# Softmaxed linear attention into an ELU feed-forward: the first two units' q in token halves, shares of their multiplies and casts on GpSimd, W1 loaded over 128 partitions, a new order table

## The chip, the cores and the metric

The kernel runs on one core of a Trainium2 chip. The core has a matrix engine (TensorE: PE, with its weight loads shown as PEld), three engines for elementwise work (VectorE: DVE; ScalarE: ACT; GpSimd: POOL), a sync engine (SP) that here only issues transfers, and 16 DMA engines that carry all transfers between the chip's memory (HBM) and the on-chip SBUF. PE writes its results to PSUM, eight banks of 512 float32 per partition; DVE and ACT read them there.

The metric is the device time in microseconds (us) of one execution: 300.37 us, the median of three runs (300.27 to 300.63).

## What is computed

The reference, cut to what matters. q, k and v have the shape (8 batches, 8 heads, 576 tokens, 64), w_in (512, 2048), w_out (2048, 512), all float32.

```
q_s = exp(q - max(q, over d));       q_s = q_s / sum(q_s, over d)
k_s = exp(k - max(k, over tokens));  k_s = k_s / sum(k_s, over tokens)
kv  = einsum('bhsd,bhse->bhde', k_s, v)
a   = einsum('bhsd,bhde->bhse', q_s, kv)
x   = a with its heads side by side: 4608 tokens x 512
h   = x @ w_in
g   = where(h > 0, h, exp(min(h, 0)) - 1)
out = g @ w_out
```

## The kernel before

**Units and blocks.** The attention is cut into 16 units, two for each batch: unit n holds four heads of batch n // 2. Its q, k and v are each one tile of 128 partitions by 2 x 9 x 64 float32 (1152 elements in a partition, 576 KB): two heads by nine chunks of tokens by 64 channels. The tokens, 4608 of them, are also cut into nine blocks of 512 for the feed-forward.

**A unit's steps.** ACT takes the exponential of q (L357). DVE sums it over the channels (L377), takes the reciprocal (L381) and multiplies (L385) into QS, in float16. PE transposes QS chunk by chunk (L408) into PSUM, from where ACT or DVE copies it to qsT (L415, L418). ACT takes the exponential of k (L361) and v is cast to bfloat16 into VB (L370 on ACT, L373 on DVE or GpSimd). PE multiplies the two into kv (L461, 36 small matmuls), DVE divides kv by the sums of k into MBLK (L470, L474), PE multiplies MBLK with qsT (L504 or L492, called "ao" below), and the result is copied into XT (L526 on ACT, L529 on DVE), the transposed x.

**The feed-forward.** W1 holds w_in as 128 partitions by four slices (kc) by 2048 columns, W2 holds w_out. For a block, eight groups g of 256 columns each take eight matmuls of 512 columns (L562: two halves by four slices kc), then exp on ACT (L578), and on ACT and DVE what makes the ELU of it (L589, L591, L595, L597), into GT. Four output tiles of a block each take sixteen matmuls against W2 (L607), a copy out of PSUM (L639) and two stores. The units of batch 0 come first, since all else needs them; the remaining units are worked off in between the matmuls of the blocks.

**The start.** `program` loads q, k, v of units 0 and 1 from SP in the order q0, k0, q1, v0, k1, v1. Ten loads of W1 go through GpSimd's queue, behind a gate: the first waits for the load of q1. Each fills 64 partitions, every second one, with rows of the upper or the lower half of w_in (`h`), for one, two or four slices kc: groups 0 to 2 for kc 0, kc 1 and kc 2 to 3, groups 3 to 4 and groups 5 to 7 for all kc. Behind them in the same queue come q2, W2 slices 0 and 1, q3, v2, k2, W2 slices 2 and 3, k3 and v3. While PE waits for the first units it runs spare matmuls on the identity (L687), from `SPIN_FROM` on.

**Order.** A planner records every operation with its reads and writes; the table ORDER, a list of operation numbers for each engine, says in which order each engine runs its operations, and the planner puts in the semaphore waits that the reads and writes ask for. An engine runs its list strictly in order: an operation that waits holds up all behind it. Durations in the code serve the planner's picture alone; on the chip the table and the waits decide.

Of the kernel before, what the change touches and what calls it, by code (L numbers as in the profile page):

```python
# [17 lines left out]
CH = 9  # L18
BYDMA = 4
CASTS = 6  # L20
CAST0, CAST1 = "act", "split"
# [3 lines left out]
        "30 32 34 47 45 49 50 53 71 73 74 58 57 72 75 77 80 78 81 76 79 82 92 96 103 125 113 100 139 "  # L25
        "138 146 147 140 148 117 141 149 119 160 159 136 161 144 166 142 168 162 167 150 169 163 156 "
        "183 185 182 184 243 249 248 247 254 253 202 255 261 259 260 266 211 267 213 273 272 265 222 "
        "271 278 277 279 323 319 230 331 343 335 327 348 360 344 290 339 292 401 409 356 301 352 422 "
        "309 405 427 361 448 418 410 489 414 372 423 431 435 374 440 436 444 383 510 449 391 493 515 "
        "497 498 506 502 460 536 462 519 523 511 528 574 471 532 524 479 595 582 578 537 587 600 591 "  # L30
        "583 548 621 608 613 550 604 596 646 559 617 609 654 650 566 622 667 672 659 655 680 663 632 "
        "693 668 634 676 698 681 689 685 719 642 706 644 702 694 711 724 715 732 707 737 728 720 745 "
        "741 750 733 771 758 754 746 763 776 759 767 784 772 789 780 785 797 793 798 802 803 807 815 "
        "811 819 "),
    "act": (
        "3 24 25 35 26 33 31 36 46 37 51 59 83 86 87 89 93 94 97 104 105 107 114 126 127 129 101 102 "
        "108 118 137 130 143 176 170 145 173 189 164 157 179 215 240 241 186 190 198 244 250 251 283 "
        "201 256 262 263 212 225 268 214 221 274 223 275 227 224 228 324 280 320 294 231 332 336 304 "
        "328 289 365 303 291 345 349 340 293 300 307 402 376 357 302 306 353 386 310 406 371 428 362 "
        "388 385 411 419 389 415 373 453 424 432 490 375 382 437 464 384 445 441 450 392 494 459 474 "  # L40
        "507 516 476 461 503 499 473 470 520 512 463 541 529 552 472 477 533 575 525 480 579 562 538 "
        "561 588 547 601 626 584 564 592 549 551 558 605 614 597 647 618 560 610 565 567 636 623 651 "
        "673 660 656 631 664 633 669 635 677 641 699 690 686 682 643 703 695 712 716 645 725 708 729 "
        "738 721 751 742 734 755 747 764 760 768 777 773 781 790 786 794 799 804 808 816 812 820 822 "),
    "dve": (
        "4 2 5 6 0 7 27 28 29 39 40 41 42 43 48 44 38 52 54 55 56 60 84 85 88 90 91 95 98 99 106 110 "
        "115 111 116 112 132 133 134 128 120 121 122 151 152 153 165 158 192 193 194 242 187 188 216 "
        "245 246 203 217 204 252 205 218 206 207 257 208 258 264 284 285 269 286 270 276 281 321 322 "
        "232 282 295 233 296 337 234 338 235 297 236 329 237 330 366 346 367 341 347 342 368 358 377 "
        "359 354 378 355 407 311 408 312 313 363 314 364 315 316 379 412 413 420 421 425 454 426 455 "  # L50
        "433 434 438 439 456 446 447 465 451 393 466 452 394 395 396 495 397 398 496 467 508 509 500 "
        "501 521 522 513 542 514 553 534 535 543 481 526 482 544 483 527 580 484 485 581 486 539 554 "
        "540 555 585 627 593 594 586 606 628 607 598 599 619 620 611 612 629 568 652 569 624 625 637 "
        "570 653 638 571 657 572 573 658 639 665 666 670 671 678 679 691 692 683 684 704 696 705 697 "
        "717 718 709 710 730 731 722 723 743 744 735 736 756 748 749 757 761 762 769 770 774 775 782 "
        "783 787 788 795 796 "),
    "gp": (
        "1 14 15 16 17 18 19 20 21 22 23 63 61 62 67 65 64 66 70 68 109 69 123 135 154 124 131 155 "
        "191 196 199 "),
    "sp": (  # L60
        "8 9 10 11 12 13 197 178 195 171 172 181 200 180 177 175 209 219 210 174 220 226 229 325 287 "
        "288 238 239 305 298 333 334 326 299 351 308 369 350 404 317 318 370 387 429 381 380 417 390 "
        "416 403 430 457 492 458 443 399 442 491 400 468 469 504 475 505 531 517 530 478 488 487 545 "
        "518 576 546 557 590 556 602 589 577 616 563 649 630 648 615 603 640 661 662 674 687 675 713 "
        "688 727 726 700 701 714 752 765 753 739 740 791 766 779 778 800 801 805 806 792 810 817 818 "
        "809 813 814 821 "),
# [17 lines left out]
class Sched:  # L84
# [5 lines left out]
    SPIN_FROM = 7900.0  # L90
# [154 lines left out]
class Gen:  # L245
# [67 lines left out]
    def load(self, n, t, key, eng="gp", follow=None):  # L313
        S = self.S
        b, u = n // 2, n % 2
        src = self.src[t][b].rearrange(
            "(h u f) (p c) d -> u (f p) h (c d)", h=2, u=2, c=CH)[u]
        tile, name = self.raw(t, n)
        dst = tile[:, :, :, :].rearrange("p h c d -> p h (c d)")
        S.add(eng, ISSUE[eng], lambda e: e.dma_start(dst, src), key, W=[name],  # L320
              dma=f"{name}{eng}", nbytes=128 * 4608,
              follow=self.gpq if eng == "gp" and n < 4 else follow)
        S.ops[-1].margin = 300 if n < 4 else 800
# [7 lines left out]
    def load_w1(self, g0, g1, kcs, key, after=()):  # L331
        w = self.w_in.rearrange("(h kc d) f -> h d kc f", h=2, d=D)
        sl = slice(g0 * 256, g1 * 256)
        ks = slice(kcs[0], kcs[-1] + 1)
        for h in range(2):
            self.S.add("gp", ISSUE["gp"], lambda e, h=h: e.dma_start(  # L336
                self.W1[h:128:2, ks, sl], w[h, :, ks, sl]), key,
                W=[f"W1_{g}{x}{h}" for x in kcs for g in range(g0, g1)],
                dma=f"w1{g0}{kcs[0]}{h}", nbytes=(len(kcs) * (g1 - g0) << 16) * (1.25 if g0 == 3 else 1), after=after,
                follow=self.gpq)  # L340
            self.gpq = self.S.ops[-1]
            self.gpq.margin = 600

    def load_w2(self, s, key, after=()):
        w = self.w_out.rearrange("(jj p) c -> p jj c", p=128)
        sl = slice(s * 4, (s + 1) * 4)
        self.S.add("gp", ISSUE["gp"], lambda e: e.dma_start(self.W2[:, sl, :], w[:, sl, :]), key,
                   W=[f"W2_{s}"], dma=f"w2{s}", nbytes=1 << 20, after=after, follow=self.gpq)

    def stage1(self, n, key, vconv="gp", what="qk"):  # L350
# [5 lines left out]
        if "q" in what:  # L356
            S.add("act", t_act(1152, False), lambda e: e.activation(flat(q), flat(q), AF.Exp),  # L357
                  key - 3, X=[f"qR{i}"], follow=self.table)
        if "k" in what:
# [4 lines left out]
            for eng, h0, h1, x in {"gp": [("gp", 0, 2, "")], "act": [("act", 0, 2, "")],  # L364
                                   "dve": [("dve", 0, 2, "")],
                                   "split": [("act", 0, 1, ""), ("dve", 1, 2, "x")]}[vconv]:
                dst, src = VB[:, h0:h1, :, 0:D], v[:, h0:h1, :, :]
                if eng == "act":
                    S.add("act", t_act(576 * (h1 - h0), False), lambda e, dst=dst, src=src:
                          e.activation(dst, src, AF.Copy), key - 50, R=[vname], W=[f"VB{i}{x}"])  # L370
                else:
                    S.add(eng, 1053 if eng == "gp" else t_dve(576 * (h1 - h0)),
                          lambda e, dst=dst, src=src: e.tensor_copy(dst, src), key - 50,  # L373
                          R=[vname], W=[f"VB{i}{x}"])
        if "q" not in what:
            return
        S.add("dve", t_dve(1152), lambda e: e.tensor_reduce(  # L377
            self.ZQ[i][:, :, :].rearrange("p h c -> p (h c)"),
            q[:, :, :, :].rearrange("p h c d -> p (h c) d"), AX.X, ALU.add),
            key - 3, R=[f"qR{i}"], W=[f"ZQ{i}"], follow=self.cleared)  # L380
        S.add("dve", 184, lambda e: e.reciprocal(self.RZQ[i][:, :, :], self.ZQ[i][:, :, :]),  # L381
              key - 3, R=[f"ZQ{i}"], W=[f"RZQ{i}"])
        rz = self.RZQ[i][:, :, :].unsqueeze(3).broadcast_to([128, 2, CH, D])
        qso = self.QS[self.alt(n)][:, :, :].rearrange("p c (h d) -> p h c d", h=2)
        S.add("dve", t_dve(1152), lambda e: e.tensor_tensor(  # L385
            qso, q[:, :, :, :], rz, ALU.mult),
            key - 3, R=[f"qR{i}", f"RZQ{i}"], W=[f"QS{self.alt(n)}"])
# [6 lines left out]
    def tp(self, n, ps, key, engs=("act", "act"), after=()):  # L394
# [7 lines left out]
        for (c0, c1, at, X, W), eng in zip(cuts, engs):  # L402
# [7 lines left out]
            S.add("pe", (c1 - c0) * 54 + 10, mm, key, R=[f"QS{self.alt(n)}", "ID"], X=X, side=1)  # L410
# [10 lines left out]
    def turn(self, n, key):  # L421
# [4 lines left out]
            key - 60, R=[f"QS{self.alt(n)}"], W=["QT"], dma="tq", nbytes=128 * 4608)  # L426
# [22 lines left out]
    KV = 382  # L449

    def kv_mm(self, n, ps, at=KV):
# [12 lines left out]
        return 615 if at == self.KV else 350, [f"kR{i}", f"VB{i}", f"VB{i}x", f"VBone{i}"], mm  # L464
# [73 lines left out]
    def early(self, g):  # L538

        names = [("QS1", 0, 2304), ("qsT10", 4096, 8704), ("qsT11", 4096, 8704),  # L540
# [6 lines left out]
    def hg_mm(self, j, g, ps, key, half=None, kc=None):  # L547
# [8 lines left out]
        ws = [f"W1_{g}{x}{h}" for x in kcs for h in range(2)]  # L556
# [97 lines left out]
    def program(self):  # L654
# [3 lines left out]
        self.gpq = None  # L658
        for n, t in ((0, "q"), (0, "k"), (1, "q"), (0, "v"), (1, "k"), (1, "v")):
            self.load(n, t, -40, "sp", follow=self.gpq)  # L660
            self.gpq = S.ops[-1]
            if (n, t) == (1, "q"):
                gate = S.ops[-1]
# [218 lines left out]
```

## Time and profile before

| what | value |
|---|---|
| median of three runs | 300.37 us |
| profiled execution, first to last instruction (its span) | 299.3 us |
| PE busy | 287.9 us (96%) |
| ACT, DVE, POOL busy | 181.3, 187.5, 22.8 us |
| first matmul against W1 (L562) | starts at 15.39 us |
| W1 loads issued on POOL | 8.65 to 14.7 us |
| moved by DMA in all | 49.96 MB |
| mean granted TensorE clock | 0.999 of full |

The page gives the profiled execution by its span; what of a run's time lies outside first to last instruction is the difference to the median, 1.07 us. Times in a timeline are us from the start of the span. A line of a group names line, engine, operation, the tiles written and read, the shape and the count, then busy time and the mean of one, then the engine's idle time just before and what ended it. The chain of waits is followed back from the last instruction: at each step to what released it. Line numbers are those of the kernel before; in the changed kernel the same code stands some lines lower (L562 becomes L576, L607 becomes L621, L336 becomes L339).

### The profile page before, as it was taken

To read this page: it belongs to the slowest core of one execution; us is meant where nothing else is said; L and a number is where in the kernel's file an instruction comes from. 1 tells how busy PE (TensorE), PEld (TensorE's weight loads), DVE (VectorE), ACT (ScalarE), POOL (GpSimd) and SP (SyncE) were. 2 spreads that over 40 slices of the span, in tenths; PEclk is the share of its full clock that TensorE was granted. 3 is DMA by queue.
4 is the path that set the end of the run, shared out by engine and by line. 5 is a ranking of instruction groups with operands and counts; after the bars stand their busy time and mean duration, and the time that the engine had idled before them with its cause. 6 is when DMAs were issued, how large, how long until landed. Compare 5 with 4: busy or idle time off the path is not lost.

```text
span 299.3 us, 4430 instructions
## 1 busy us (share of the span) xinstructions
PE 287.9 (96%) x1856; PEld 234.4 (78%) x1856; DVE 187.5 (63%) x244; ACT 181.3 (61%) x212; POOL 22.8 (8%) x35
## 2 busy tenths in 40 slices
PE   0999999999999999999999999999999999999995
PEld 0487877778888888888888888888888888888885
DVE  3858944997588767678468656749743654465500
ACT  5758749989788776674776576644553343334221
POOL 0880235100000000000000000000000000000000
PEclk9999999999999999999999999999999999999999
DMA  7999998997796795519626852450401130030433
GB/s 263 383 360 391 387 392 299 251 243 273 126 346 169 160 321 128 149 40 305 144 92 174 274 132 58 114 94 1 94 0 35 37 88 18 0 70 2 99 76 88
DMA packets 35475, 49.96 MB, mean 167 GB/s; under 512 B 16384, under 2 KB 16640, under 8 KB 35456
## 3 DMA queue, kind: packets, MB, share of 16 engines
q1 hardware_dynamic: 29840, 34.15, 41.8%
q0 software_dynamic: 5536, 15.47, 15.9%
q8 instruction: 14, 0.23, 0.3%
q10 hardware_dynamic: 80, 0.07, 0.1%
q14 instruction: 5, 0.04, 0.0%
HBM read 36.70 MB, written 9.44 MB: 154 GB/s over the span
## 4 chain that ended last, share of the span: by engine, by line
PE 84%; DMA 6%; DVE 4%; ACT 3%; POOL 2%; SPq 0%; issue 0%
PE PS L607 42%; PE PS L562 38%; DMA W<-in_moe_w_in_dram 4%; PE PS L492 2%; DMA QR<-in_q_dram 2%; POOL W L336 2%; PE PS L461 1%; DVE GT L597 1%; DVE GT L591 1%; ACT QR L357 1%; ACT OSBX L639 1%; DVE ESB L595 1%; DVE QS L385 0%; DVE ZQ L377 0%; ACT ESB L589 0%; DVE MBLK L474 0%
## 5 line engine op out<-in xcount | busy, mean ns | idle before, releaser
L562 PE MATMUL PS<-XT,W 128*128 128x512 f32 x576 | 139.8, 392 | 0.7 <-DVE GT L597 0.6
L607 PE MATMUL PS<-W,GT 128*128 128x512 f32 (+1 forms) x592 | 140.1, 386 | 0.0
L562 PEld LDWEIGHTS PS<-XT,W 128*128 128x128 f32 x576 | 106.8, 188 | 23.7 <-DVE GT L597 1.0
L607 PEld LDWEIGHTS PS<-W,GT 128*128 128x128 f32 x592 | 108.0, 188 | 21.6 <-DVE GT L591 0.3
L578 ACT ACTIVATE ESB<-PS 128x1024 f32<-128x1024 f32 x72 | 73.3, 1027 | 68.1 <-PE PS L562 67.6
L595 DVE TENSOR_SCALAR ESB<-ESB 128x1024 f32<-128x1024 f32 x64 | 44.2, 690 | 72.6 <-ACT ESB L578 72.4
L597 DVE TENSOR_TENSOR GT<-ESB,PS 128x1024 fp32r<-128x1024 f32 x64 | 77.5, 1215 | 1.6
L639 ACT ACTIVATE OSB<-PS 128x512 f32<-128x512 f32 x31 | 18.6, 599 | 23.3 <-PE PS L607 18.2
L526 ACT ACTIVATE XT<-PS 128x512 fp32r<-128x512 f32 (+6 forms) x32 | 19.4, 608 | 12.7 <-PE PS L492 7.7
L377 DVE TENSOR_REDUCE ZQ<-QR 128x18 f32<-128x1152 f32 x16 | 21.6, 1347 | 5.7 <-ACT QR L357 5.7
L385 DVE TENSOR_TENSOR QS<-QR,RZQ 128x1152 f16<-128x1152 f32 x16 | 21.6, 1352 | 0.8 <-PE PS L408 0.6
L357 ACT ACTIVATE QR<-QR 128x1152 f32<-128x1152 f32 x16 | 18.7, 1170 | 3.5 <-DMA QR<-in_q_dram 3.5
L361 ACT ACTIVATE KR<-KR 128x1152 bf16<-128x1152 f32 x16 | 18.3, 1161 | 2.5 <-DMA KR<-in_k_dram 2.5
L370 ACT ACTIVATE VB<-VR 128x1152 bf16<-128x1152 f32 (+1 forms) x12 | 13.5, 1124 | 1.7 <-PE PS L461 1.3
L436 ACT ACTIVATE qsT<-QT 128x1152 fp32r<-128x1152 f16 x12 | 14.0, 1170 | 0.0
L492 PEld LDWEIGHTS PS<-qsT,MBLK 128*128 128x128 f32 x60 | 11.0, 190 | 2.5 <-DVE MBLK L474 0.2
L492 PE MATMUL PS<-qsT,MBLK 128*128 128x320 f32 (+4 forms) x60 | 12.5, 296 | 0.0
L687 PE MATMUL PS<-ID 128*128 128x512 f16 x12 | 4.6, 508 | 7.3 <-ACT KR L361 7.3
L591 DVE SCALAR_TENSOR_TENSOR GT<-PS,ESB 128x1024 fp32r<-128x1024 f32 x8 | 9.8, 1222 | 2.8 <-ACT ESB L589 2.7
L474 DVE TENSOR_TENSOR MBLK<-PS,RZK 64x128 fp32r<-64x128 f32 x32 | 9.2, 286 | 0.7
L589 ACT ACTIVATE ESB<-ESB 128x1024 f32<-128x1024 f32 x8 | 8.5, 1059 | 0.2
L461 PEld LDWEIGHTS PS<-VB,KR 64*64 64x64 bf16 x576 | 5.7, 109 | 3.0 <-ACT VB L370 0.8
(31 smaller groups left out, 59.3 us busy)
## 6 DMA issues: line engine op xcount, KB each, us to landing
out_dram<-OSB SPq DMA_DIRECT2D x62, 128.0 KB, 2.4
QR<-in_q_dram SPq DMA_DIRECT2D x12, 576.0 KB, 4.5
KR<-in_k_dram SPq DMA_DIRECT2D x12, 576.0 KB, 5.7
VR<-in_v_dram SPq DMA_DIRECT2D x12, 576.0 KB, 4.6
W<-in_moe_w_out_dram POOLq DMA_DIRECT2D x4, 1024.0 KB, 18.4
QR<-in_q_dram POOLq DMA_DIRECT2D x4, 576.0 KB, 11.3
VR<-in_v_dram POOLq DMA_DIRECT2D x4, 576.0 KB, 9.6
KR<-in_k_dram POOLq DMA_DIRECT2D x4, 576.0 KB, 14.7
```

Source lines behind the costliest of these rows:

```text
L357: S.add("act", t_act(1152, False), lambda e: e.activation(flat(q), flat(q), AF.Exp), key - 3, X=[f"qR{i}"], follow=self.table)
L361: S.add("act", t_act(1152, False), lambda e: e.activation(ek[:, :, :, :].rearrange("p h c d -> p (h c d)"), flat(k), AF.Exp), key - 2, X=[ ...
L377: S.add("dve", t_dve(1152), lambda e: e.tensor_reduce(self.ZQ[i][:, :, :].rearrange("p h c -> p (h c)"), q[:, :, :, :].rearrange("p h c d ...
L385: S.add("dve", t_dve(1152), lambda e: e.tensor_tensor(qso, q[:, :, :, :], rz, ALU.mult), key - 3, R=[f"qR{i}", f"RZQ{i}"], W=[f"QS{self.al ...
L492: last = e.matmul(P[:, y:y + n_], M[:, f, :], T[:, c0:c1, f * 64:f * 64 + 64], start=True, stop=True)
L526: S.add("act", t_act((h1 - h0) * n_, True), lambda e, dst=dst, src=src: e.activation(dst, src, AF.Copy), key, W=W, X=X)
L562: last = e.matmul(P[:, t * 512:(t + 1) * 512], self.W1[:, kc, tt * 128:(tt + 1) * 128], self.XT[:, kc, rc:rc + BLK], start=(kc == 0), stop ...
L578: S.add("act", t_act(1024, True), lambda e: e.activation(esb[:, :], P[:, :], AF.Exp), key, W=[f"E{i}"], X=banks)
L595: S.add("dve", t_dve(1024, 2), lambda e: e.tensor_scalar(esb[:, :], esb[:, :], 1.0, -1.0, ALU.min, ALU.add), key, X=[f"E{i}"])
L597: S.add("dve", t_dve(1024), lambda e: e.tensor_tensor(gt, esb[:, :], P[:, :], ALU.max), key, R=[f"E{i}"], W=gw, X=banks)
L607: last = e.matmul(dst, GT[:, jj, ts * 128:(ts + 1) * 128], self.W2[:, jj, c0:c1], start=(jj == 0), stop=(jj == 15))
L639: S.add("act", t_act(512, True), lambda e: e.activation(osb[:, :], src, AF.Copy), key, W=[f"O{i}0", f"O{i}1"], X=[f"b{bk}"])
```

## The change

- The q of units 0 and 1 is worked in two parts: chunks 0 to 4 (640 elements in a partition) and 5 to 8 (512): exponential, sum, reciprocal and multiply each once for each part. The multiply of the second part runs on GpSimd. All later units keep one operation each.
- The v casts of units 0 and 1 are split by chunks: 0 to 4 on ACT, 5 to 8 on GpSimd. Before, ACT cast all of unit 0; ACT cast one head and DVE the other of unit 1.
- The first loads are issued in the order q0, q1, k0, v0, k1, v1, and the gate of the W1 loads is k0's load.
- W1 is loaded by twelve DMAs of 128 partitions, one slice kc each (384 KB for groups 0 to 2 and 5 to 7, 256 KB for 3 to 4). In each, neighbouring partitions hold rows of the upper and the lower half of w_in.
- In GpSimd's queue the two multiplies stand ahead of all W1 loads, the two casts between them; then W2 slice 0, q2, W2 slice 1, q3, k2, v2, W2 slices 2 and 3, the cast of v2, k3 and v3.
- The spare matmuls may begin at 5.5 us of the planner's time instead of 7.9, and the order table is a new one on every engine.

```diff
-CAST0, CAST1 = "act", "split"
+CAST0, CAST1 = "pair", "pair"
+XT0, XT1, TP0, TP1 = "both", "both", ("act", "act"), ("act", "dve")
...
-    SPIN_FROM = 7900.0
+    SPIN_FROM = 5500.0
...
+    HALF = ((0, 5), (5, CH))
...
     def load_w1(self, g0, g1, kcs, key, after=()):
-        w = self.w_in.rearrange("(h kc d) f -> h d kc f", h=2, d=D)
+        w = self.w_in.rearrange("(h kc d) f -> d h kc f", h=2, d=D)
         sl = slice(g0 * 256, g1 * 256)
-        ks = slice(kcs[0], kcs[-1] + 1)
-        for h in range(2):
-            self.S.add("gp", ISSUE["gp"], lambda e, h=h: e.dma_start(
-                self.W1[h:128:2, ks, sl], w[h, :, ks, sl]), key,
-                W=[f"W1_{g}{x}{h}" for x in kcs for g in range(g0, g1)],
...
+        for kc in kcs:
+            self.S.add("gp", ISSUE["gp"], lambda e, kc=kc: e.dma_start(
+                self.W1[:, kc, sl], w[:, :, kc, sl]), key,
+                W=[f"W1_{g}{kc}" for g in range(g0, g1)],
...
-                                   "split": [("act", 0, 1, ""), ("dve", 1, 2, "x")]}[vconv]:
-                dst, src = VB[:, h0:h1, :, 0:D], v[:, h0:h1, :, :]
+                                   "pair": [("act", 0, 5, ""), ("gp", 5, 9, "y")]}[vconv]:
+                if vconv == "pair":
+                    dst, src = VB[:, :, h0:h1, 0:D], v[:, :, h0:h1, :]
...
+        for c0, c1, xs in ([(c0, c1, [x]) for x, (c0, c1) in enumerate(self.HALF)]
+                           if n in self.HALVED else [(0, CH, [0, 1])]):
+            part, m = slice(c0, c1), (c1 - c0) * 128
+            qp, zp, rp = q[:, :, part, :], self.ZQ[i][:, :, part], self.RZQ[i][:, :, part]
+            if n in self.HALVED:
+                S.add("act", t_act(m, False), lambda e, qp=qp: e.activation(qp, qp, AF.Exp),
...
+            S.add("dve", t_dve(m), lambda e, qp=qp, zp=zp: e.tensor_reduce(zp, qp, AX.X, ALU.add),
...
+            S.add("dve", 184, lambda e, zp=zp, rp=rp: e.reciprocal(rp, zp),
...
+            eng = "gp" if n in self.HALVED and c0 else "dve"
+            S.add(eng, m * 2.2 + 80 if eng == "gp" else t_dve(m), lambda e, qp=qp, rz=rz, dst=qs[:, :, part, :]: e.tensor_tensor(
+                dst, qp, rz, ALU.mult),
...
+    HALVED = (0, 1)
...
-        for n, t in ((0, "q"), (0, "k"), (1, "q"), (0, "v"), (1, "k"), (1, "v")):
-            self.load(n, t, -40, "sp", follow=self.gpq)
-            self.gpq = S.ops[-1]
-            if (n, t) == (1, "q"):
+        for n, t in ((0, "q"), (1, "q"), (0, "k"), (0, "v"), (1, "k"), (1, "v")):
+            self.load(n, t, -40, "sp")
+            if (n, t) == (0, "k"):
                 gate = S.ops[-1]
-        loaded = S.ops[-1]
-        for g0, g1, kcs in ((0, 3, (0,)), (0, 3, (1,)), (0, 3, (2, 3)), (3, 5, range(4)), (5, 8, range(4))):
-            self.load_w1(g0, g1, kcs, -30, [gate, self.ident] if kcs == (0,) else ())
-            S.ops[-2].behind = loaded
+        self.load_w1(0, 3, (0,), -30, [gate])
+        self.load_w1(0, 3, (1, 2, 3), -30)
+        self.load_w1(3, 5, range(4), -30)
+        self.load_w1(5, 8, range(4), -30)
...
+        self.load(2, "q", -28)
         self.load_w2(0, -29)
         self.load_w2(1, -29)
-        for t in "qkv":
-            self.load(2, t, -28)
+        for n, t in ((2, "k"), (2, "v"), (3, "q")):
+            self.load(n, t, -28)
         self.load_w2(2, -27)
-        for t in "qkv":
+        self.load_w2(3, -25)
+        for t in "kv":
             self.load(3, t, -26)
-        self.load_w2(3, -25)
```

On the engines the new table gives this for the start. DVE sums q0's second part, q1's second part, q0's first, q1's first, then multiplies the two first parts. ACT takes the four exponentials, copies q0's second part out of PSUM, then k0, v0, k1, q0's first part, v1, the first XT copy, q1's first part, the next XT copy. PE transposes the second parts of units 0 and 1, the first part of unit 0, does unit 0's kv, transposes the first part of unit 1, ao of unit 0, kv of unit 1, four matmuls of W1's slice 0 (groups 0 and 1), ao of unit 1, and then slice by slice. Before, six matmuls of W1 (slices 0 and 1) stood ahead of ao of unit 1.

## The prediction

> **What bounds the kernel now.** I read the page's busy shares first, then the chain of waits in order of time up to 60 us, then the timeline of the first 22 us, then one-microsecond windows of the DMA rate, then the DMA issues.
>
> ```profile
> PE 287.9 (96%) x1856; PEld 234.4 (78%) x1856; DVE 187.5 (63%) x244; ACT 181.3 (61%) x212; POOL 22.8 (8%) x35
> ```
>
> PE is busy 96% of the span, and in the long middle (100 to 250 us) 100% at full clock. A gain can only come from where PE isn't yet on real work, or waits.
>
> ```profile
> 1.75 6.62 DMA QR<-in_q_dram
> 8.65 5.38 POOL W L336 x9
> 14.03 11.32 DMA W<-in_moe_w_in_dram
> 25.35 0.04 issue
> 25.39 5.74 PE PS L562 x24
> ...
> 53.85 1.22 DVE GT L591
> ...
> 56.93 1.26 DVE ZQ L377
> ...
> 58.83 1.22 DVE GT L597
> ```
>
> Start and length in us. The chain of the first 25 us isn't arithmetic: it is q of unit 1 landing (the gate of the W1 loads), nine W1 issues on POOL, and the last W1 transfer, which lands at 25.35 us; the 24 matmuls behind it (groups 5 to 7) start at once. The waits put 0.52 us of idle weight load down to it. Near 54 to 60 us the chain runs through DVE, with a q reduction (1.26 us) inside it.
>
> ```profile
> 13.84 0.29 DVE L474 TENSOR_TENSOR MBLK<-PS,RZK 64x128 fp32r<-64x128 f32 x1
> 14.16 0.76 DVE L373 CAST VB<-VR 128x576 bf16<-128x576 f32 x1
> 14.19 0.73 PE L504 MATMUL PS<-qsT,MBLK 128*128 128x512 f32 x2 [0.18 <-DVE MBLK L474]
> 14.72 0.60 ACT L526 ACTIVATE XT<-PS 128x512 fp32r<-128x512 f32 x1
> 14.96 0.69 DVE L529 CAST XT<-PS 128x512 fp32r<-128x512 f32 x1
> 14.98 0.48 PE L461 MATMUL PS<-VB,KR 64*64 64x65 bf16 x36
> 15.39 1.66 PE L562 MATMUL PS<-XT,W 128*128 128x512 f32 x6
> ```
>
> Real work starts at 15.39 us, when XT of unit 0 is there. PE is full from then to 25 us.
>
> ```profile
> 14.00:15.00 1.00, 0.76 (x7) 0.32 (x6) 0.93 (x3) 0.95 (x3) 1.00 (x3) 1.00 1.03 347
> 15.00:16.00 1.00, 1.00 (x39) 0.87 (x40) 0.97 (x3) 0.32 (x1) 1.00 (x2) 1.00 0.84 276
> 16.00:17.00 1.00, 1.00 (x6) 0.82 (x5) 0.34 (x2) 0.00 (x0) 1.00 (x3) 1.00 0.97 258
> 17.00:18.00 1.00, 1.00 (x6) 0.83 (x5) 0.68 (x1) 0.45 (x1) 1.00 (x2) 1.00 1.15 324
> 18.00:19.00 1.00, 1.00 (x6) 0.68 (x6) 0.02 (x1) 0.15 (x1) 1.00 (x3) 1.00 1.25 408
> ```
>
> The last number is GB/s. The transfers run at 390 to 410 from 3 to 13 us and again from 18 to 47 us; between lies a hole: 341, 347, 276, 258, 324. Against 400 it lacks 59 + 53 + 124 + 142 + 76 = 454 KB, worth 1.1 us of a stream that everything to 47 us stands in line for.
>
> ```profile
> W<-in_moe_w_in_dram POOLq DMA_DIRECT2D x2, 768.0 KB, 10.6
> W<-in_moe_w_in_dram POOLq DMA_DIRECT2D x4, 192.0 KB, 4.5
> ```
>
> The first four W1 loads move 192 KB each and land 4.4 to 4.7 us after issue: they land about 0.55 us apart, as POOL issues them (0.62 us each, so 317 GB/s). The hole begins there.
>
> **The change, part by part.** Profiled span 299.3 us; the median is 300.37, so 1.07 us lies outside first to last instruction. I leave that unchanged and take terms off the median.
>
> *Landings.* From issue and time to landing: q0 4.64, k0 6.05, q1 8.35, v0 9.86, k1 11.31, v1 12.8 us. With q1 now second I take 6.05 for it and 8.35 for k0.
>
> *q in halves.* An exp of 1152 takes 1.17; by the evictions of 512 and 640 (0.60, 0.70) the halves take 0.63 and 0.73. ACT: q0 from 4.63 to 5.88, q1 from 6.08 to 7.33. DVE reductions by the 512 copy (0.69) and in proportion 0.68 and 0.82, reciprocals 0.17 to 0.27. The changed order puts q1's 512 half ahead of q0's 640 half, so DVE waits from 6.2 to 6.75, with the 640 half behind it. Then q1's half to 7.67, the 640 halves' reductions to 9.6, the two DVE multiplies (0.82 each by 1.35/1152) to 10.44 and 11.54. Before, QS1 was complete at 12.62: DVE is 1.1 us earlier.
>
> *Multiplies on GpSimd.* No two-input operation on POOL is in the trace. Nearest rows: its cast, 1.146 us for 1152 (0.51 for 512), and its affine select, 0.282 for 128 (1.13 for 512). I take 1.13, as the nearer to a computing operation, and 0.51 as the lower end; above, the sum of both rows, 1.64. So 6.3 to 7.45 and 7.8 to 8.95. Behind them in POOL's queue stand all W1 issues: 8.95 against 8.65. Even at 1.64 they start at 9.6 us; kc 0 (now 384 KB) lands some 4.8 later, at 13.8 to 14.4, before PE wants it. The Trainium skill speaks against this part: "GPSIMD Engine Reference", section 3.1, has about 2.6 cycles an element for two inputs (an estimate of 1.1 us here) and section 4.1 says to keep such work on the Vector engine. By it the sum stays, since POOL idled there. Section 8 adds contention with Vector instructions of two SBUF inputs; here POOL casts took 1.142 to 1.159 us beside such an instruction and beside none.
>
> *v casts.* POOL takes 512 of each 1152 (0.51 us), ACT 640 (about 0.73). That takes 0.76 off DVE and 0.4 off ACT for unit 0. POOL reaches them at about 10.25 and 12.75 us, when v0 and v1 have landed or are about to; ten and seven W1 issues stand behind.
>
> *The path to the first real matmul.* ACT now: transpose half out, k0's exp (from 9.05), v0 (to 10.85), k1's exp from its landing 11.31 to 12.5, second half of qsT out to 13.1, v1 to 13.75. PE: cold spare matmuls take 0.49, warm 0.28; through 13 spares and three transposes it reaches unit 0's kv at 12.0 to 12.3. DVE makes MBLK by 13.3 to 13.75 (reciprocal 0.55 behind kv, as before, then 0.17 and twice 0.28). So the two matmuls of L504 run at 13.4 to 13.8 instead of 14.19, XT 0.4 to 0.8 earlier, and the first W1 matmul at 14.6 to 15.0. Given back: its second pair is in the bank that ACT must first empty of unit 1's qsT (0.70, behind the XT copy), and unit 1's ao comes after four matmuls instead of six: 0.15 to 0.25. I take 0.5 us for the start, bounds 0.15 and 0.9.
>
> *W1 by 128 partitions.* Twelve issues for ten, with two casts between: POOL ends them at 8.95 + 12 x 0.65 + 2 x 0.55 = 17.9 us instead of 14.7. Issues of 256 to 384 KB per 0.65 us supply 400 to 600 GB/s, so the hole from the supply side closes. If all 454 KB come back the last W1 lands 1.1 earlier, at 24.2; if none, 25.35; a loss is the slower rival below. PE, 0.5 us earlier, wants groups 5 to 7 at 25.39 - 0.48 - 0.5 = 24.4. So the stall of 0.48 goes and the start's 0.5 holds: 0.98 us.
>
> *q2, W2 and the rest* are issued from 18 us on instead of 14.6. This costs nothing while W1 still fills the queue to 24 us; without that cover it would be their 3.4 us. W2 slice 2 landed at 39.45, 0.36 us before PE wanted it, and k2 at 36.75 led without slack to kv at 39.4; so the gain holds only if the stream itself is earlier. k2 is now before v2 in the queue. k3 and v3 are issued behind v2's cast, near 38 us: hidden by the W2 slices (landed 39.45 and 42.2). kv of unit 3 stands four matmuls (0.9 us) earlier; ready at 46.45 by the old landing, wanted at 46.67 less the gain: the same condition.
>
> *New order, 45 to 60 us.* DVE's q reduction now stands before the group's L605, while ACT still evicts: 1.26 us leave the chain of 54 to 60 us. PE's losses there are small (0.3 over 32 matmuls, 0.25, 0.28), so I take 0.2, bounds 0 and 0.8. Behind 60 us, 235.9 us hold 234.9 us of work by the row's 0.227 per matmul: a new order can cost or give 0.5; I take 0.
>
> Sum: 0.5 + 0.48 + 0.2 = 1.18; 300.37 - 1.18 = 299.2 us.
>
> **Rivals.** *The stream is no earlier* (the hole isn't supply). For: between 15 and 17 us supply was already 384 KB per issue and the rate stayed at 276 and 258. Then W1 lands at 25.3, groups 5 to 7 start 0.1 earlier, and with the order's 0.2 the time is 300.1. The early start is hidden anyway. Chance 0.2.
>
> *The new W1 pattern is slower.* Each load now alternates between the two halves of w_in, 2 MiB apart (256 rows of 8 KB). The slowest W1 load of before, at 384 KB in 1.55 us, ran at 254 GB/s; kept for 4.19 MB from 12.3 us that ends at 28.8, PE 3.4 us late: 303.5. Before averaged 4.19 MB in 13.05 us, 321 GB/s; below that it decides, below 306 it costs over 0.6 us; at 295 the time is 301.2. Against: the single-slice loads ran as fast as supplied. The Trainium skill speaks for it: "DMA: Bandwidth & Descriptors", section "Latency and other measured facts", has copies with a row pitch of 2 MiB fall to 164 GB/s; by that estimate W1 takes 25.5 us and the kernel loses over 12. Only one step in two has that pitch here, the rest 8 KB, so I follow the trace. Chance 0.19.
>
> *POOL gates.* If a multiply takes over 2.7 us, kc 0 lands after 16.5 and PE starts a microsecond later than before: about 301, more with the W1 tail. The rows give 1.64 at most. With a table that adds stalls behind 60 us: 0.08.
>
> **How the numbers follow.** A measurement of this kernel can tell about 0.2% (0.6 us). Forecast 0.53: faster by more, time 299.2, own range 298.4 to 299.8. Same 0.2, slower 0.19 + 0.08 = 0.27. The range: below, 0.9 + 0.48 + 0.8 would be 298.2, taken at 298.3; above, into the slower rivals to 301.3.
>
> **What would show it.** First W1 matmul at 14.6 to 15.0; POOL multiply near 1.13 us; DMA rate near 390 in 14 to 18 us; last W1 before 24.5 and no PE wait for it; DVE's reduction out of the chain near 57 us. Wrong if W1 lands after 25.4, if POOL's first W1 issue is after 10.5, or if PE shows new waits behind 60 us.

## The result and the profile after

The changed kernel took 300.4 us (median of 20 runs, 300.04 to 301.07), the kernel before, beside it, 301.08 us (20 runs, 300.27 to 302.03). The ratio is 0.9981, with a 95% interval of 0.9973 to 0.999: a gain of 0.57 us (0.68 between the medians), where 1.18 was forecast (a ratio of 0.9961). Measured a second time, with 12 runs, the ratio was 0.9969 (0.9952 to 0.9987), a gain of 0.93 us. So it is faster, by half of what the sum said in the first measurement and by four fifths in the second, whose interval holds the forecast. The forecast time, 299.2 us, is 1.2 below the measured one; 0.7 of that is the kernel before, which took 301.08 here and not the 300.37 of three runs. The profiled span went from 299.3 to 299.0 us, and the tables below explain that 0.3. The profiled execution of the changed kernel, at 300.83 us, was one of its longer ones; a second profile, with a span of 298.7, is read with the experiments.

The page of the changed kernel, first the busy line, then the matmul group of W1 with PE's idle time ahead of it:

```profile
PE 289.4 (97%) x1860; PEld 235.2 (79%) x1860; DVE 186.5 (62%) x247; ACT 181.3 (61%) x214; POOL 27.9 (9%) x41
...
L576 PE MATMUL PS<-XT,W 128*128 128x512 f32 x576 | 139.8, 392 | 1.0 <-DMA W<-in_moe_w_in_dram 1.0
```

POOL has 5 us more work, DVE 1 us less. The second line holds the answer already: PE stands idle for 1.0 us, and a W1 load ends that wait. The timeline of PE (start, length in us) says which load:

```profile
13.27 0.70 PE L518 MATMUL PS<-qsT,MBLK 128*128 128x512 f32 x2 [0.20 <-DVE MBLK L488]
...
14.55 1.20 PE L576 MATMUL PS<-XT,W 128*128 128x512 f32 x4
15.59 0.70 PE L518 MATMUL PS<-qsT,MBLK 128*128 128x512 f32 x2
16.12 4.70 PE L576 MATMUL PS<-XT,W 128*128 128x512 f32 x20
21.83 9.39 PE L576 MATMUL PS<-XT,W 128*128 128x512 f32 x40 [1.00 <-DMA W<-in_moe_w_in_dram]
```

The first W1 matmul starts at 14.55 us instead of 15.39. Counted where both kernels have ao of units 0 and 1 behind them: the fifth W1 matmul starts at 16.12, and before, the seventh started at 17.36, two matmuls (0.45) further on, so the start gained 17.36 - 0.45 - 16.12 = 0.79 us. But 4 + 20 matmuls are groups 0 to 2, and the wait of 1.00 us follows right behind them: it is for groups 3 and 4. By count it costs 21.83 - (16.12 + 20 x 0.227) = 1.17 us. The kernel before had no wait at this place; its own, by the same count, was 25.39 - (17.36 + 34 x 0.227) = 0.31 us, ahead of groups 5 to 7. So 0.79 + 0.31 - 1.17 = -0.07: at 25 us nothing is left of the earlier start. The matmuls of groups 5 to 7 start at 25.46 (25.39 before), and the block that starts at 49.64 before starts at 49.72.

The chain of waits in order of time (start, length, what) names the cause of that wait:

```profile
3.51 9.13 DMA VR<-in_v_dram
12.63 0.05 issue
12.69 0.62 POOL VB L378
13.31 0.36 POOL W L339
13.66 0.10 issue
13.76 0.87 POOL W L339 x2
14.63 0.17 issue
14.80 6.98 DMA W<-in_moe_w_in_dram
21.78 0.04 issue
21.83 9.39 PE PS L576 x40
```

v of unit 1 lands at 12.64 us, POOL casts its part, then issues more W1 loads; the fourth of them is issued at 14.80 and lands 6.98 us later, at 21.78. What stands between is written in the order table: behind the second cast GpSimd issues one of groups 5 to 7 (384 KB) ahead of three of groups 3 and 4.

The hole in the DMA rate is closed all the same. One-microsecond windows: busy time of PE, PEld, DVE, ACT and POOL, then granted clock, DMA share, GB/s.

```profile
13.00:14.00 1.00, 0.80 (x4) 0.40 (x3) 0.82 (x2) 0.75 (x2) 1.00 (x3) 1.00 1.23 406
14.00:15.00 1.00, 1.00 (x39) 0.67 (x38) 0.95 (x3) 0.97 (x2) 1.00 (x3) 1.00 1.21 399
15.00:16.00 1.00, 1.00 (x6) 0.70 (x5) 0.46 (x2) 0.00 (x0) 1.00 (x4) 1.00 1.23 387
16.00:17.00 1.00, 1.00 (x6) 0.83 (x5) 0.68 (x1) 0.60 (x1) 1.00 (x4) 1.00 1.29 409
17.00:18.00 1.00, 1.00 (x6) 0.81 (x5) 0.02 (x1) 0.00 (x0) 1.00 (x3) 1.00 1.27 382
```

The rate was 347, 276, 258 and 324 GB/s from 14 to 18 us before, and is 399, 387, 409 and 382 now. The bytes come earlier, but not in the order in which PE asks for them.

Further on, DVE's reductions of q have left the chain; where before it ran through DVE from 54 to 66 us, it is now PE almost throughout:

```profile
49.88 7.42 PE PS L576 x32
57.30 0.71 PE PS L475 x72
58.01 2.04 PE PS L621 x8
60.04 0.04 issue
60.08 3.96 PE PS L576 x16
...
81.17 2.95 PE PS L576 x13
```

From the block that starts at 49.72 to the one that starts at 81.17 it is 31.45 us; before, 49.64 to 81.50 was 31.86. (Here and below the first time is from PE's timeline and the second from the chain, which puts the same start 0.16 to 0.17 us later, in all kernels alike.) So this stretch gains 0.41. With -0.07 at 25 us that makes the 0.3 of the span; behind 81 us the two kernels keep step (the last 88 matmuls start at 279.46 and 279.72).

### The profile page after: what moved, and what is told of

It is laid out like the page before. It is cut to its first block, busy times and chain, and to the rows that moved or that the text cites. A ratio compares the mean times of both kernels' runs of the same rounds, so it can differ in the third digit from the quotient of the medians.

```text
span 299.0 us, 4453 instructions
## 1 busy us (share of the span) xinstructions
PE 289.4 (97%) x1860; PEld 235.2 (79%) x1860; DVE 186.5 (62%) x247; ACT 181.3 (61%) x214; POOL 27.9 (9%) x41
## 4 chain that ended last, share of the span: by engine, by line
PE 92%; DMA 5%; SPq 1%; POOL 1%; issue 0%; ACT 0%
PE PS L621 44%; PE PS L576 43%; DMA VR<-in_v_dram 3%; PE PS L506 3%; DMA W<-in_moe_w_in_dram 2%; PE PS L475 2%; SPq L322 1%; POOL W L339 0%; PE PS L421 0%; POOL VB L378 0%; ACT OSB L631 0%
## 5 line engine op out<-in xcount | busy, mean ns | idle before, releaser
L621 PE MATMUL PS<-W,GT 128*128 128x512 f32 (+1 forms) x592 | 140.4, 386 | 0.0
L576 PEld LDWEIGHTS PS<-XT,W 128*128 128x128 f32 x576 | 106.9, 188 | 24.4 <-DMA W<-in_moe_w_in_dram 1.4
L621 PEld LDWEIGHTS PS<-W,GT 128*128 128x128 f32 x592 | 107.9, 188 | 21.4 <-DVE GT L605 0.4
L390 DVE TENSOR_REDUCE ZQ<-QR 128x18 f32<-128x1152 f32 (+2 forms) x18 | 21.8, 1208 | 5.1 <-ACT QR L388 4.3
L397 DVE TENSOR_TENSOR QS<-QR,RZQ 128x1152 f16<-128x1152 f32 (+1 forms) x16 | 21.0, 1310 | 0.1
L358 ACT ACTIVATE QR<-QR 128x1152 f32<-128x1152 f32 x14 | 16.4, 1169 | 0.0
L699 PE MATMUL PS<-ID 128*128 128x512 f16 x16 | 6.9, 559 | 5.4 <-ACT QR L388 5.4
L484 DVE RECIPROCAL RZK<-PS 128x2 f32<-128x2 f32 x16 | 2.6, 160 | 8.6 <-PE PS L475 7.5
```

The lines of the kernel that those rows point to most:

```text
L390: S.add("dve", t_dve(m), lambda e, qp=qp, zp=zp: e.tensor_reduce(zp, qp, AX.X, ALU.add), key - 3, R=[f"qR{i}{x}" for x in xs], W=[f"ZQ{i}{ ...
L397: S.add(eng, m * 2.2 + 80 if eng == "gp" else t_dve(m), lambda e, qp=qp, rz=rz, dst=qs[:, :, part, :]: e.tensor_tensor(dst, qp, rz, ALU.mult),
L576: last = e.matmul(P[:, t * 512:(t + 1) * 512], self.W1[:, kc, tt * 128:(tt + 1) * 128], self.XT[:, kc, rc:rc + BLK], start=(kc == 0), stop ...
L621: last = e.matmul(dst, GT[:, jj, ts * 128:(ts + 1) * 128], self.W2[:, jj, c0:c1], start=(jj == 0), stop=(jj == 15))
```

## The experiments

Two theories were set against each other at first. One: the wait for groups 3 and 4 eats the start, and an order of the W1 loads that follows PE would give it back. The other: the gain sits in the new order of 50 to 80 us alone, and start and W1 bring nothing. All ratios are against the kernel before, run beside it. In the experiments the same code stands some lines lower again; the tiles tell which it is. A change of the start also changes how many spare matmuls the planner puts in; in e4, e6, e7, e8, e9 and the second kernel of e1 their number was set by a small table, so that the starts stay alike.

**e1: the W1 loads in PE's order.** In GpSimd's list 14 to 17 are groups 0 to 2, 18 to 21 groups 3 and 4, 22 to 25 groups 5 to 7, 28 and 44 the casts. Only the place of 25 changes:

```diff
-        "1 36 52 14 15 28 16 17 20 44 25 18 21 19 23 22 24 ...
+        "1 36 52 14 15 28 16 17 20 44 18 21 19 25 23 22 24 ...
```

> The changed kernel with one W1 load moved in GpSimd's queue: slice 3 of groups 5 to 7 goes behind all four loads of groups 3 to 4 instead of between them. Theory (the 1.0 us wait of PE at 21 us in the changed kernel comes from that load, whose 384 KB take 1.0 us of the transfers, standing ahead of groups 3 to 4): the wait shrinks from 1.0 to 0.3 us or less, groups 5 to 7 start at 24.5 to 24.9 us instead of 25.45, and the time falls by 0.4 to 0.9 us against the changed kernel, to a ratio of 0.995 to 0.997 against the kernel before. Rival A (the 128-partition loads as such land late, because the engines run out of step): groups 3 to 4 still land after 21.5 us and the time stays within 0.2 us of the changed kernel. Rival B (what follows is as tight): the wait goes but comes back at groups 5 to 7 or at a W2 slice, and the time stays.

> The kernel of e1_w1_order once more, as the partner of the others in this call and for more runs. Expected by the theory: ratio 0.994 to 0.997 against the kernel before, PE's wait for groups 3 to 4 at 0 to 0.5 us.

Measured: 299.65 us (5 runs), ratio 0.9957 (0.9944 to 0.9969); again, 299.6 us (6 runs), 0.9952 (0.9937 to 0.9967). PE's wait for W1 was 0.3 us in the first profile (span 298.3) and nothing in the second (span 297.6), whose timeline of PE is this:

```profile
14.10 1.20 PE L585 MATMUL PS<-XT,W 128*128 128x512 f32 x4
15.14 0.70 PE L527 MATMUL PS<-qsT,MBLK 128*128 128x512 f32 x2
15.67 14.03 PE L585 MATMUL PS<-XT,W 128*128 128x512 f32 x60
```

Sixty matmuls of W1 stand without a gap where the changed kernel had 20, a wait, and 40. The place of one load in a queue is worth 0.12 to 0.29% (0.9981 and 0.9969 against 0.9957 and 0.9952), about 0.4 to 0.9 us. Against the first measurement of the changed kernel the intervals lie apart, against the second (0.9952 to 0.9987) they overlap.

**e2 and e3: the new order from 52 us on, taken out of the changed kernel and put alone into the one before.** Only the lists of PE, ACT, DVE and SP behind that point change (69 places in e2). On DVE, in e2 (227 to 229 are the reduction, reciprocal and multiply of a later unit's q; among the others are the block's ELU and the division of kv):

```diff
-        "205 227 253 198 199 228 256 214 257 215 216 263 217 229 ...
+        "205 253 198 199 227 256 257 214 228 215 263 216 229 217 ...
```

> The changed kernel with the order of before on every engine from about 52 us on (14 places differ on PE, 15 on ACT, 21 on DVE, 19 on SP). Theory (what the change gained, about 0.3 us in the profiled spans, came from the new order between 60 and 80 us, and the start gave nothing in the end): PE's progress at 80 us falls back by 0.25 to 0.35 us and the time is within 0.25 us of the kernel before. Rival (the gain came from the start): the time stays that of the changed kernel, ratio 0.998 against the kernel before.

> The kernel before with the changed kernel's order from about 52 us on, the start untouched. Theory (the gain sits in that order): faster than the kernel before by 0.25 to 0.6 us, ratio 0.998 to 0.9992, with the start as before (first W1 matmul at 15.4, last W1 at 25.35). Rival (it sits in the start): no difference to the kernel before, ratio 0.9995 to 1.0005.

Measured: e2 300.61 us, ratio 0.9987 (0.9977 to 0.9997), and 31.99 us from its block at 49.02 to the one at 81.01 (31.45 in the changed kernel). e3 301.53 us, 1.0011 (1.0002 to 1.002), 32.22 us for that stretch, in a profile with a mean granted clock of 0.951. So the new order is not a gain of its own: with the old start it brought nothing. The theory that the gain sits in the order alone falls; and e2, whose interval lies below 1, speaks for a gain of the start and W1 without the new order, though a small one.

**e4: the ten old W1 loads in the changed kernel.** `load_w1` and its calls as before, in groups' order:

```diff
-        w = self.w_in.rearrange("(h kc d) f -> d h kc f", h=2, d=D)
+        w = self.w_in.rearrange("(h kc d) f -> h d kc f", h=2, d=D)
...
-                self.W1[:, kc, sl], w[:, :, kc, sl]), key,
+                self.W1[h:128:2, ks, sl], w[h, :, ks, sl]), key,
```

> The changed kernel with W1 loaded as before, by ten DMAs of 64 partitions, the casts at the like places between them and the same numbers of spare matmuls. Theory (the hole in the transfer rate at 13 to 18 us belongs to the old loads, which supply 192 KB per issue): the rate falls to 250 to 350 GB/s between 13 and 18 us again, the last W1 lands after 25.3 us, PE waits 1 to 2 us in all for W1 between 16 and 26 us, and the time is 0.3 to 1.5 us above the changed kernel. Rival (the hole came from something else at the start, such as the gate or the order of the first loads): the rate stays near 400 and the time that of the changed kernel or better.

Measured: 301.62 us, ratio 1.0018 (1.0009 to 1.0027). The same windows as above:

```profile
13.00:14.00 1.00, 0.43 (x3) 0.30 (x3) 0.97 (x2) 0.52 (x1) 1.00 (x3) 1.00 0.86 270
14.00:15.00 1.00, 1.00 (x28) 0.49 (x30) 0.35 (x2) 0.56 (x2) 1.00 (x3) 1.00 0.92 221
15.00:16.00 1.00, 1.00 (x39) 0.76 (x24) 0.93 (x4) 0.64 (x2) 1.00 (x2) 1.00 1.07 370
16.00:17.00 1.00, 1.00 (x5) 0.67 (x4) 0.18 (x2) 0.26 (x1) 1.00 (x3) 1.00 0.88 235
17.00:18.00 1.00, 1.00 (x6) 0.82 (x5) 0.66 (x1) 0.34 (x1) 1.00 (x2) 1.00 1.05 258
```

The hole is back (270, 221, 370, 235, 258), and groups 5 to 7 wait for W1 again, until 25.53, though for 0.4 us and not the 1 to 2 expected. The experiment isn't clean at the start: with other loads ahead of it in POOL's queue, unit 0's cast came later and PE waited 0.94 us for it, so that the first W1 matmul ran at 15.21, 0.66 later than in the changed kernel. How much of the loss is that start and how much the layout, this run doesn't separate. Its profiled span, 299.2, shows less of a loss than its median does (its profiled execution, at 301.01 us, was also faster than that median).

**The changed kernel again, and e5: the twelve new W1 loads alone, in the kernel before.**

> The changed kernel once more, beside the other kernels of this call, for a second profile of the wait for W1 and a second ratio. Theory: first W1 matmul at 14.3 to 14.6 us, a wait of PE for groups 3 to 4 of 0.4 to 1.2 us (it was 1.0 in one profile and 0.5 in the variant with the old tail, with the same start), ratio 0.997 to 0.999. Rival (the ratio of 0.998 was chance): 1.000.

> The kernel before with W1 alone loaded by twelve DMAs of 128 partitions, in plain order; q, casts and order as before. Theory (the layout closes the hole in the transfers, but the start waits for arithmetic): 380 GB/s or more from 13 to 18 us, the last W1 lands at 24.3 to 24.9 us, PE's wait for it (0.3 to 0.5 us) goes, the first W1 matmul stays at 15.3 to 15.5, and the time falls by 0.2 to 0.5 us: ratio 0.998 to 0.9995. Rival (a hole of supply has no price at all): the ratio stays 1.000.

> The kernel before with W1 alone loaded by twelve DMAs of 128 partitions, once more, since the first profile was of a disturbed run. Theory: 380 GB/s or more from 13 to 18 us, the last W1 lands before 24.9 us, PE's wait for it goes, the first W1 matmul stays at 15.3 to 15.5 us, ratio 0.998 to 0.9995. Rival (a hole of supply has no price): ratio 1.000 and the same PE times at 49 us.

The changed kernel: 300.17 us, ratio 0.9969 (0.9952 to 0.9987), span 298.7. Two lines of PE's timeline differ from the first profile:

```profile
21.05 9.37 PE L576 MATMUL PS<-XT,W 128*128 128x512 f32 x40 [0.40 <-DMA W<-in_moe_w_in_dram]
...
57.21 0.78 PE L475 MATMUL PS<-VB,KR 64*64 64x65 bf16 x72 [0.67 <-POOL VB L378]
```

The wait for groups 3 and 4 is 0.4 us (0.56 by count, as the fifth W1 matmul starts at 15.95). So groups 5 to 7 start at 21.05 + 16 x 0.227 = 24.68, and the first 25 us gain 0.71, not -0.07. Then the order's gain is missing: PE waits 0.67 us at 57 us for POOL's cast of a later unit's v, and from the block at 48.94 to the one at 80.81 it is 31.87 us, as in the kernel before. The two executions of one program thus gain in different places.

e5: 301.24 us, 0.9992 (0.9976 to 1.0009); again, 301.16 us, 1.0002 (0.999 to 1.0014). In the second profile of e5 the hole is closed (387, 396, 389, 391, 393 GB/s from 13 to 18 us), PE waits for no W1 load, and yet the block that starts at 49.64 in the kernel before starts at 49.78. The reason is the start, not the layout: the spare matmuls ran slower.

```profile
11.89 1.46 PE L690 MATMUL PS<-ID 128*128 128x512 f16 x3
...
15.93 1.66 PE L566 MATMUL PS<-XT,W 128*128 128x512 f32 x6
```

Three spare matmuls took 1.46 us here and 0.85 in the kernel before (11.93 to 12.78), and the first W1 matmul came at 15.93 instead of 15.39. So the layout alone brings nothing that can be measured; how much it would bring without that later start this run doesn't say.

**e6: q of unit 1 third again.** Loads in the order q0, k0, q1, all else as changed:

```diff
-        "8 9 10 11 12 13 ...
+        "8 10 9 11 12 13 ...
```

> The changed kernel with the first loads again in the order q0, k0, q1. Theory (GpSimd's queue is a chain: q1's landing, exp, sum, multiply, then every W1 load): q1 lands at 8.35 instead of 6.1, GpSimd's second multiply ends at 11.1 to 11.3 instead of 8.9, all W1 loads are issued 2.2 us later, the first W1 matmul comes at 15.8 to 16.5 us, the last W1 lands after 25.5, and the time is 0.8 to 2.2 us above the changed kernel. Rival (the transfers are backed up, so that issuing later costs nothing): the time rises by less than 0.4 us.

Measured: 302.43 us, ratio 1.0046 (1.0024 to 1.0067), span 301.3. POOL's timeline:

```profile
10.28 1.05 POOL L406 TENSOR_TENSOR QS<-QR,RZQ 128x512 f16<-128x512 f32 x1 [3.00 <-DVE RZQ L402]
11.27 1.35 POOL L348 DMA_DIRECT2D W<-in_moe_w_in_dram  x2
...
```

The second multiply waits 3.00 us for DVE, and W1's first issue, behind it in POOL's queue, goes out at 11.27 instead of 8.84 us. The first W1 matmul starts at 17.18, 2.6 us later than in the changed kernel, with DMA rates of 75, 323, 218 and 243 GB/s from 12 to 16 us. A late operation on POOL does move the whole W1 stream, so the early q of unit 1 is what makes room for multiplies there. The loss isn't that of the stream alone: PE itself waits 1.84 us for this multiply, at 11.39. Another part is the clock: its windows show 0.84 of full from 12 to 13 us and 0.50 from 13 to 16.

**e7: e1 with the multiplies of both second parts on DVE.**

```diff
-            eng = "gp" if n in self.HALVED and c0 else "dve"
+            eng = "dve"
...
-        "1 36 52 14 15 28 ...
+        "1 14 15 28 ...
```

> The kernel of e1_w1_order with the two multiplies of the second parts on DVE instead of GpSimd, each right behind its reciprocal; 16 spare matmuls, placed for it. Theory (GpSimd's multiplies bring little, since DVE waits 0.6 us for q1 anyway and what is left is absorbed before kv): W1 issues begin at 8.4 instead of 8.88 us, MBLK is done at most 0.4 us later, and the time is within 0.35 us of e1_w1_order. Rival (DVE is the bound of the start): the first W1 matmul comes 0.7 to 0.9 us later and the time rises by 0.6 to 0.9 us against e1_w1_order.

Measured: 299.71 us, ratio 0.9957 (0.994 to 0.9974), the ratio of e1. W1's first issue is at 8.32, the first W1 matmul at 14.36, and PE waits for no W1 load. The profile's span, 299.6, is long for another reason:

```profile
58.14 0.77 PE L484 MATMUL PS<-VB,KR 64*64 64x65 bf16 x72 [1.60 <-POOL VB L387]
```

At 58 us PE waits 1.60 us for POOL's cast of a later unit's v; the changed kernel shows no such wait in its first profile and 0.7 us in its second. That is an exposure of the new order (unit 4's and 5's kv now stand ahead of eight matmuls of L621); the changed kernel, without e7's edit, shows it too.

**e8: e1 with the order of before from 52 us on.** The same exchange as in e2.

> The kernel of e1_w1_order with the order of before from about 52 us on, where the kv of units 4 and 5 stands behind eight matmuls of the feed-forward instead of ahead of them. Theory (the new order's early kv is a chance that it doesn't always get: v of unit 5 lands between 54.7 and 56.9 us, and its cast and with it kv wait for that, 0.7 us in one profile and 1.6 in another): no wait of PE for GpSimd's cast, and a time within 0.3 us of e1_again, since the old order loses 0.4 elsewhere. Rival (the new order is better by the 0.4 to 0.5 us that the profiles of the changed kernel and of e2_after_oldtail show between 49 and 81 us): 0.4 to 0.6 us slower than e1_again.

Measured: 300.49 us, ratio 0.9978 (0.9965 to 0.9992), against 0.9952 of e1 beside it. From its block at 48.46 to the one at 80.31 it is 31.85 us; in e1, 48.29 to 79.76, 31.47. So with the new start the new order is worth 0.4 us in the profiles and 0.26% in the ratios.

**e9: e1 with the v casts as they were before.**

```diff
-CAST0, CAST1 = "pair", "pair"
+CAST0, CAST1 = "act", "split"
```

DVE's share of unit 1's v stands ahead of the XT copy; in GpSimd's list the two casts are gone.

> The kernel of e1_w1_order with the v casts of units 0 and 1 as before: ACT all of unit 0, ACT one head and DVE the other of unit 1, DVE's cast ahead of its XT copy. Theory (the casts on GpSimd are what takes the work off DVE in front of XT): ACT loses nothing for unit 0 (it waits for k1 anyway), DVE's cast of 0.76 us delays kv of unit 1 and DVE's XT copy, the first W1 matmul comes at 14.7 to 15.2 instead of 14.16, and the time rises by 0.3 to 0.6 us. Rival (the W1 loads, now issued up to 1.1 us earlier as no cast stands among them, set the pace): the start is later but the time stays within 0.2 us or falls.

Measured: 299.48 us, ratio 0.9949 (0.9934 to 0.9964). DVE's timeline shows where the cast went:

```profile
12.37 0.69 DVE L441 CAST qsT<-PS 128x512 fp32r<-128x512 f16 x1
13.10 0.76 DVE L388 CAST VB<-VR 128x576 bf16<-128x576 f32 x1
13.78 0.69 DVE L553 CAST XT<-PS 128x512 fp32r<-128x512 f32 x1
```

It fits into a gap that DVE has anyway: the XT copy behind it starts at 13.78, and the first W1 matmul at 14.32. So the casts on GpSimd bring nothing either, in sum: without them the W1 loads are also issued earlier (the last at 14.85 instead of 16.10 us), and the two effects aren't separated.

e1 and e9 beat both kernels: 299.5 to 299.65 us, 0.43 to 0.51% faster than before.

## Why the forecast was too high

**The step that failed** is "PE, 0.5 us earlier, wants groups 5 to 7 at 25.39 - 0.48 - 0.5 = 24.4. So the stall of 0.48 goes and the start's 0.5 holds: 0.98 us." The last W1 load was indeed early (issued at 16.36 us, landed at 24.72), and nothing waited for it. But it was the only load that was set against PE's demand; a wait for groups 3 and 4 was put at nothing without a reason. They are wanted at 20.66, right behind groups 0 to 2, and their last load was issued at 14.80 behind a load of groups 5 to 7 that PE wants 16 matmuls, 3.6 us, later. In the kernel before they landed at 20.46 (issued at 12.82), with PE wanting them at 17.36 + 18 x 0.227 = 21.45: 1.0 us of slack. The start took 0.79 of it, and in the new queue they landed 21.78 - 20.46 = 1.32 us later; that is the wait of 1.17 by count. e1 shows it: one load three places further back, and the wait goes or shrinks to 0.3. Instead of 0.98 us the first 25 us gave -0.07 in the first profile and 0.71 in the second. The stall of 0.48 that was to go was also too large: by count it was 0.31.

The order table alone would not have given that wait. The loads of W1 land 0.98 us apart at 384 KB and 0.67 apart at 256 KB, but the one of groups 5 to 7 in question landed 2.52 us after the one ahead of it. At the regular pace groups 3 and 4 would have landed, by an estimate, at 17.23 + 0.98 + 3 x 0.67 = 20.2 us, before PE wanted them. So two things add up: the load in the wrong place, and a delay of 1.5 us (0.7 in the second profile) that the last section reads. e1 takes only the first away.

**The start** was right in its working and too small: 0.79 us instead of 0.5, within its bounds of 0.15 and 0.9 (0.96 in the second profile, just outside). kv of unit 0 ran at 11.77 (12.0 to 12.3 said), MBLK was done at 13.12 (13.3 to 13.75), the first W1 matmul ran at 14.55 (14.6 to 15.0).

**GpSimd's terms** were right in size: the multiplies took 1.05 us at 6.34 and 7.85 (1.13 from 6.3 and 7.8 said), W1's first issue came at 8.84 (8.95), its last ended near 17.6 (17.9). The estimate by the Trainium skill's "GPSIMD Engine Reference", section 3.1, was 1.1 us, as near. What the prediction didn't ask was whether they are needed: beside e1's order of loads, e7 and e9 give the same time with that work on DVE and ACT, so this part of the change neither gains nor costs anything that can be measured.

**The layout of W1** did what was said on the DMA rate, but not for the reason given, so that this was in part luck. The prediction puts the hole down to supply, to loads issued too slowly. In the kernel before, all ten were issued by 14.7 us, and the view of DMA from 0 to 17 us has this for their queue (packets, MB, share):

```profile
q0 software_dynamic: 738, 1.84, 34.1%
```

So 1.84 of W1's 4.19 MB had moved, and between 15 and 17 us, at 276 and 258 GB/s, more than half of it stood in the queue. Nor did the first four loads land 0.55 us apart, as issued, but 0.46 to 0.49. e4 and e5 show that the layout makes and closes the hole; whether by the 64 partitions of a load or by its several slices no run separates. The rival of a slow pattern is refuted: 382 to 409 GB/s, where the rule in the Trainium skill's "DMA: Bandwidth & Descriptors", section "Latency and other measured facts", on a row pitch of 2 MiB would have given 164. No run here has that pitch between all rows, so the rule itself wasn't tried. "The stream is no earlier", with its 300.1, came near the measured time, but by luck: the stream was earlier, its order was not PE's.

**The order of 45 to 60 us** was mis-sized: 0.4 us instead of 0.2 in the first profile and in both of e1, within its bounds, and nothing in the second profile, where PE waits for the v cast; in e7's profile, with a wait of 1.60 us, it lost. In the ratios only e8 shows it. By these profiles its worth hangs on when a later unit's v lands (5.3 to 7.8 us after issue there), a wait that the prediction didn't price. With the old start e3 shows none of it; why is not settled. Behind 60 us the 0 was right.

The 1.07 us that was set between span and median is not what lies outside the span: wherever a run has both numbers, its time exceeds its span by 1.8 to 1.9 us, so the profile of before shows an execution of some 301.1 us. The forecast gain isn't touched by it.

The parts depend on each other: the layout alone 1.0002, the new order alone 1.0011, all but the layout 1.0018 (with a later start), all but the new order 0.9987, all together 0.9981 and 0.9969, and with one load moved 0.9957 and 0.9952. The new start by itself, without layout and order, wasn't tried.

## What to carry to other kernels

When a start becomes earlier, check every later delivery against the new demand, group by group, and not just the one that was late before. In a queue that is filled to the end, the order of the loads counts beside their rate. And where a change has several parts, measure them without each other and together: here neither the layout nor the order gained anything alone, with the new start both seem to, and the work on GpSimd could have been left out. Take more than one profile: two executions of one program lost their time in different places.

## What was not expected of the hardware

- *A load lands after its bytes could be there.* The last load of groups 3 and 4 landed at 21.78 us; by then the stream had moved some 7.6 MB, and 6.55 MB stood in the queues up to and with it: about 1.05 MB, at 400 GB/s some 2.6 us, went to loads behind it. A count of bytes ahead of a load is thus a lower bound for its landing here, not its time.
- *One small transfer stands by that delay.* The view of DMA from 17 to 18 us shows, in the first profile, a single packet of another kind among the loads:

```profile
q8 instruction: 1, 0.02, 7.0%
```

It is 16 KB, starts at 17.46 us and takes 1.1 us. In nine profiles with the twelve loads (all but the first of e5, and e6 with its late issues) exactly one load lands 0.7 to 1.6 us later than the regular pace, and always 2.2 to 2.8 us after the start of such a packet; the loads behind it follow at the regular pace, so the delay stays. The packet starts at 17.46 and 16.94 us in the two profiles of the changed kernel, at 16.96 and 15.97 in those of e1. That it causes the delay is not shown: no run moved it.

- *The delay varies.* In the same program the wait for groups 3 and 4 was 1.0 us in one execution and 0.4 in the next, in e2 0.5.
- *Spare matmuls don't become faster at the same moment.* Three took 1.46 us in one program and 0.85 in another at the same place, with the granted clock at 1.00 in both. It moved the first W1 matmul by half a microsecond, as much as the term that was to be measured.
- *POOL's cast of 512 elements* took 0.62 to 0.95 us; the 0.51 of the prediction is the 1.146 us of 1152 elements in proportion, and no cast of 512 ran on POOL before.
